# Smaller loads, held for a place in TensorE's program: a ReLU²-attention and gated-MLP kernel on Trainium2

## The chip, the core and the metric

The kernel runs on one core of one Trainium2 chip. A core has TensorE (PE, matmuls; its weight loads are shown apart as PEld), VectorE (DVE), ScalarE (ACT), GpSimd (POOL) and SyncE (SP), and 16 DMA engines that move data between HBM and the core's SBUF and fetch program code. POOL and SP each issue DMAs in the order of their own program. The metric is device time in microseconds (us), as the median of several runs; the profile shows one execution.

## The reference

Attention without softmax, then a gated MLP without gate choice. Inputs are f32, the output is f32.

```python
batch, n_heads, seq, head_dim = (8, 12, 448, 64)
scores = 1/sqrt(64) * q @ k.T              # per batch and head
attn   = maximum(scores, 0)**2 / 448 @ v   # 8 x 12 x 448 x 64
x = attn.transpose(0, 2, 1, 3).reshape(3584, 768)
g, val = x @ w_gate, x @ w_val             # 768 -> 1536
out = (0.5*g*(1 + erf(g/sqrt(2))) * val) @ w_out   # 1536 -> 768
```

## The kernel before

Everything on TensorE is bf16 on 64x64 pieces of the array, so that four small matmuls run side by side. Each batch's 12 heads are worked in three **thirds** of four heads, named (b, m). A third goes through these steps:

- **Loads** (POOL queue). `load_qk` (line 345) issues one DMA for the four heads of q and one for those of k into the tile `qk16`, `load_v` (line 362) two for v, one for each half of the sequence; all cast f32 to bf16 on the way. `load` (line 319) makes the planned operation, with the bytes over a rate of 400e3 bytes per us as its planned transfer time (`arrivals`), and adds by hand the instructions that it must wait for (`op.behind`, reason "pace").
- **Transposition.** In batches 0 and 1 it is done by TensorE. From batch 2 on (`add_dma_transposes`, line 393), DVE regroups q and k into `qkr` (line 402) and SP issues two transposing DMAs (line 407) into `qkT`, one for four of the seven 64-row chunks and one for three. The second of a pair waits for the landing of the first; in batch 2 each waits for the one before it.
- **Scores, ReLU, square, values.** TensorE makes scores from `qkT` (tile `sp`), ACT takes the ReLU (line 634), DVE squares (line 646), TensorE multiplies with `v`, and DVE or ACT puts the result into `xT`.
- **MLP.** Gate, value and output products on `xT`, partly by seven-product Strassen groups, with gelu on ACT, sums on DVE, and output stores issued by SP (line 1156).

Buffers limit how far loads run ahead: `qk16` has two (RING_H), `v16` and `qkT` three each.

The order of every engine's instructions is made by a planner, `run_plan` (line 74), when the kernel is built. It steps through planned time. POOL and TensorE's lower rows have queues with a fixed order; SP, ACT, DVE and the upper rows have pools from which the earliest ready operation is taken. `ready` (line 84) gives the planned time at which an operation's inputs are there. TensorE work of later batches lies in a list `units`, and the first unit of the list that is ready is taken, so that other work goes ahead of a unit whose data are late. The planner counts 5.0 us for the landing of a transposing DMA after its issue, and 3.0 us more before scores may use it (1.5 us in batch 2).

Loads from batch 2 on are listed at line 1198 (`late`): q and k of one third, then v of the third before. Lines 1342 to 1350 pace them: q of third n waits for ReLU 0, and k for ReLU 1, of third n-3; the two v loads of a third wait for ReLUs 3 and 5 of the third two before it (PACE, line 252).

Of the kernel before, what the change touches and what calls it, by code (L numbers as in the profile page):

```python
# [28 lines left out]
class Op:  # L29


    def __init__(self, engine, cost, emit, deps=(), lag=0.0, prio=0, other=None):
        self.engine, self.cost, self.emit, self.prio = engine, cost, emit, prio
        self.deps = [d for d in deps if d is not None]
        self.lag = lag
        self.other = other
        self.takes = None
        self.margin = 0.0
        self.after = None
        self.start = self.end = self.known = self.blocked = None  # L40


# [15 lines left out]
            self.keys.add(key)  # L58


class Unit:


# [7 lines left out]
BANK = 0.3  # L71


def run_plan(queues, pools, units, banks, arrivals, together, fill):

    free = {e: 0.0 for e in (*queues, *pools)}
    at = {e: 0 for e in queues}
    dma = last = floor = busy = 0.0  # L80
    units.sort(key=lambda u: u.at)
    fixed = len(queues["PE0"])

    def ready(op):
        if op.known is not None:
            return op.known
        if op.blocked is not None and op.blocked.end is None:
            return None
        t = 0.0
        if op.after is not None:  # L90
            if op.after.start is None:
                return None
            t = op.after.start
        if op.takes is not None:
            x = op.takes[0].free(*op.takes[2:])
            if x is None:
                return None
            t = max(t, x)
        for d in op.deps:
            if d.end is None:  # L100
                op.blocked = d
                return None
            t = max(t, d.end + d.lag + (op.margin if d.engine == "SP" else 0.0))
        if op.takes is None:
            op.known = t
        return t
# [38 lines left out]

    left = sum(map(len, queues.values())) + sum(len(u.los) + len(u.his) for u in units)
    left += len({id(op) for ops in pools.values() for op in ops})
    while left:
        best = None
        for e, ops in queues.items():  # L150
            if at[e] < len(ops):
                r = ready(ops[at[e]])
                if r is not None:
                    t = max(r, free[e], floor if e in together else 0.0)
                    key = (t, 0, free[e])
                    if best is None or key < best[0]:
                        best = (key, e, ops[at[e]])
        whole = at["PE0"] == len(queues["PE0"])
        if whole or at["PE0"] >= fixed:
            found = next_unit(not whole)  # L160
            if found is not None:
                key = (found[0], -1, free["PE0"])
                if best is None or key < best[0]:
                    best = (key, "PE0", found)
        for e, ops in pools.items():
            mine = None
            for op in ops[:48]:
                r = ready(op)
                if r is not None:
                    t = max(r, free[e], floor if e in together else 0.0)  # L170
                    key = (t, op.prio, free[e])
                    if mine is None or key < mine[0]:
                        mine = (key, e, op)
            if mine and (best is None or mine[0] < best[0]):
                best = mine
        assert best is not None, "the plan is stuck"
        (t, _, _), e, op = best
        if isinstance(op, tuple):
            _, u, k = op
            u.begun = True  # L180
            units.remove(u)
            if k is not None:
                u.box["k"] = k
                banks[k] = u.closer()
            queues["PE0"][at["PE0"]:at["PE0"]] = u.los
            pools["PE1"] += u.his
            op = u.los[0]
        if op.other is not None and e != op.engine:
            op.engine, op.cost, op.emit = op.other
        op.start = t  # L190
        op.end = t + op.cost
        free[e] = op.end
        if e in together:
            floor = t
            if t > busy:
                fill(busy, t)
            busy = max(busy, op.end)
        if op in arrivals:
            dma = max(dma, op.end) + arrivals[op]
            op.lag = dma + 2.0 - op.end  # L200
        if e in at:
            at[e] += 1
        else:
            pools[e].remove(op)
            if op.other is not None:
                for x in ("ACT", "DVE"):
                    if x != e:
                        pools[x].remove(op)
        if op.takes is not None:
            op.takes[0].take(*op.takes[1:])  # L210
        op.emit()
        last = max(last, op.end)
        left -= 1
# [4 lines left out]
def kernel(  # L218
# [17 lines left out]
    P = 64  # L236
# [12 lines left out]
    OGS = d_model // NG  # L249
    WOG = 3  # L250
    SB = 2
    PACE = 0, 1, 3, 5
    FB = 4
    FILL = 30.0
    EARLY = 2

    NP = 2
    RING_V, RING_T, RING_H, RING_R, RING_A, RING_O = 3, 3, 2, 2, 4, 4
# [33 lines left out]
    ctx.enter_context(tc.manual_schedule())  # L292

    HALF = (slice(0, P), slice(P, 2 * P))

    n_reg, = nc.alloc_registers("n", engines=OrderedSet([mybir.EngineType.PE]))
    SYNC = mybir.DependencyInfo(mybir.DependencyClass.Sync, mybir.DependencyReason.DATA)

    def mm(o, lhsT, rhs, row, col, start, stop, onto=False):
        return nc.tensor.matmul(o, lhsT, rhs, start=start, stop=stop, skip_group_check=onto,  # L300
                                tile_position=(P * row, P * col))

    def wait_lower(box):

# [14 lines left out]
    def load(nbytes, emit, deps=(), cost=0.7, rate=400e3):  # L319
        def paced():  # L320
            ins = emit()
            for d in op.behind:
                tc.add_manual_dep(ins.ins, d.ins.name, SYNC, reason="pace")

        op = Op("POOL", cost, paced, deps)
        op.behind = [*deps]
        arrivals[op] = nbytes / rate
        POOL.append(op)
        return op
# [32 lines left out]
    def load_v(b, h0, h1, deps=()):  # L362

        m = h0 // 4
        for i in range(2):
            def emit(i=i):
                if (b, m) not in v16:
                    v16[b, m] = qkv.tile([128, 4, VC, D], bf16, name="v16", tag="v16")
                c0 = i * (SC - VC)
                return nc.gpsimd.dma_start(  # L370
                    v16[b, m][HALF[i], :, :, :],
                    v[b, h0:h1].rearrange("h (p c) d -> p h c d", c=SC)[:, :, c0:c0 + VC, :])
            op = load(4 * (h1 - h0) * VC * P * D, emit, deps, rate=400e3 if b else 300e3)
            v_loads.setdefault((b, m), []).append(op)
# [18 lines left out]
    def add_dma_transposes(b, m, deps=()):  # L393
# [9 lines left out]
                qkr[b, m].rearrange("p c h d -> p h c d"),  # L403
                qk16[b, m].rearrange("p h (c d) -> p h c d", d=D))

        def emit_transpose(c0, c1):
            ins = nc.sync.dma_start_transpose(
                qkT_tile(b, m)[:, c0:c1].rearrange("d c r x -> d (c r) x"),
                qkr[b, m][:, c0:c1].rearrange("p c h d -> p (c h d)"))
            if b > EARLY and c0 or m and b == EARLY:  # L410
                tc.add_manual_dep(ins.ins, one[0].ins.name, SYNC, reason="pace")
            one[:] = [ins]

        n = len(regrouped)
        copy = Op("DVE", 0.62, emit_copy, [wait, *(regrouped[n - 2] if n > 1 else ())], lag=0.15, prio=1)
        DVE.append(copy)
        copy.margin = 3.0
        tr_op[b, m] = [Op("SP", 0.19 * 2 * (c1 - c0), lambda c0=c0, c1=c1: emit_transpose(c0, c1),
                          [copy], lag=5.0) for c0, c1 in ((0, VC), (VC, SC))]
        qk_used[b, m] = [copy]  # L420
        t_made[b, m] = [*tr_op[b, m]]
        if m or b > EARLY:
# [51 lines left out]
    def fill(t0, t1):  # L474
# [10 lines left out]
            return  # L485
        t = new_bank(k, held[k])
        for _ in range(n):
            nc.tensor.matmul(t[:, :], warm[:, 0:128], warm[:, :], start=True, stop=True)  # L488

    last_scores = [None]  # L490

# [31 lines left out]
    def add_first_transposes(at):  # L523

        def emit(box, c0, c1, reader):
            src = qk16[0, 0].rearrange("p h (c d) -> p h c d", d=D)
            box[0] = t = new_bank(box["k"], reader, [128, c1 - c0, 2 * P], bf16)
            for c in range(c0, c1):
                for j in range(2):
                    nc.tensor.transpose(t[HALF[j], c - c0, :], src[:, j, c, :],  # L530
                                        ident[:, :], tile_position=(0, P * j))

        for engine, copy, c0, c1 in (("DVE", nc.vector.tensor_copy, 0, VC), ("ACT", nc.scalar.copy, VC, SC)):
            box = {}
# [14 lines left out]
    def add_transposes(at, b, m, rs):  # L549
# [6 lines left out]
        def emit(r):  # L556
# [7 lines left out]
            src = qk16[b, m].rearrange("p h (c d) -> p h c d", d=D)  # L564
            for c in range(SC):
                for j in range(2):
                    nc.tensor.transpose(t[HALF[j], c, :], src[:, 2 * r + j, c, :],  # L567
                                        ident[:, :], tile_position=(0, P * j))

        def emit_copy(r):  # L570
            nc.vector.tensor_copy(qkT_tile(b, m)[:, :, r, :], box[r])
# [626 lines left out]
    late = [(b, m) for b in range(2, B) for m in range(NM)]  # L1198
    for n, (b, m) in enumerate(late):
        for i in range(2):  # L1200
            load_qk(b, i, 4 * m, 4 * m + 4)
        for b_, m_ in late[n - 1:n] + (late[n:] if n == len(late) - 1 else []):
            load_v(b_, 4 * m_, 4 * m_ + 4)
    for b, m in late:
        add_dma_transposes(b, m)

# [122 lines left out]
    def emit_warm_up():  # L1329
        t = new_bank(0, None)  # L1330
        for _ in range(8):
            for j in range(2):
                nc.tensor.matmul(t[HALF[j], :], warm[:, HALF[j]], warm[:, :],
                                 start=True, stop=True, tile_position=(0, P * j))
    PE0.insert(0, warm_op)

    thirds = [(b, m) for b in range(B) for m in range(NM)]
# [4 lines left out]
    for n, (b, m) in enumerate(thirds):  # L1342
# [2 lines left out]
                op.behind.append(relus[(*thirds[n - 3], PACE[i])])  # L1345
        if (b, m) >= (2, 0):
            for i, op in enumerate(v_loads[b, m]):
                op.behind.append(relus[(*thirds[n - 2], PACE[2 + i])])
        for op in (*qk_loads[b, m], *v_loads[b, m]):
            op.deps += op.behind  # L1350
    for new, old in zip(duos[RING_A:], duos):
        gone = [o_op[b, pr] for keys in old["of"] for b, pr, _ in keys]
        for sq in new["sq"]:
# [9 lines left out]
    for op in [*ACT, *DVE]:  # L1363
        if op.other is not None:
# [1 line left out]

    banks = {k: readers.get(k, [None])[-1] for k in range(FB + 2)}
    run_plan({"PE0": PE0, "POOL": POOL}, {"PE1": PE1, "ACT": ACT, "DVE": DVE, "SP": SP, "IDLE": IDLE}, later,
             banks, arrivals, ("PE0", "PE1"), fill)


# [28 lines left out]
```

## Time and profile before

| what | value |
|---|---|
| median of 3 runs | 412.27 us (411.99 to 413.25) |
| the profiled execution, first to last instruction (span) | 410.9 us |
| TensorE busy | 395.7 us, 96% of the span |
| VectorE, ScalarE, GpSimd busy | 286.9, 243.9, 73.7 us |
| mean granted TensorE clock | 0.995 of full speed |
| DMA packets of the software queue (loads) | 37152, 24.39 MB |
| DMA packets of the hardware queue (stores, transposes) | 37888, 19.08 MB |
| DMA packets of TensorE's instruction queue (q8) | 70, 1.15 MB |
| transposing DMAs | 36, median 5.0 us from issue to landing |
| v loads; q loads; k loads of four heads | 4.6; 5.2; 6.5 us to landing (medians) |

The profile names instructions by the line that records them. All matmuls of attention and MLP are recorded at line 300 (the helper `mm`), so they are told apart by the tiles that they write and read: `sp<-qkT` are scores, `ff<-attnT,v` values, the rest the MLP. "issue" as the cause of idle time means that the engine waited for nothing that the profile shows. The packets of a DMA are shown by queue: q0 carries the loads, q1 stores and transposes, q8 and q14 program code. 1.15 MB in 70 packets is 16 KB for each.

### The profile page before, as it was taken

The numbers are of one execution on the slowest core, as the hardware profiler recorded it, in microseconds if no ns is written. First come the engines' busy times: TensorE is split into PE (matmuls) and PEld (weight loads), VectorE is DVE, ScalarE is ACT, GpSimd is POOL, SyncE is SP. The second block draws the span as 40 slices with busy tenths as digits, with TensorE's granted clock in tenths as the row PEclk, the third lists the DMA queues.
The fourth block names the chain that finished last, engine by engine and source line by source line (L and its number), as shares of the span: only waits on it lengthen the run. The fifth ranks groups of instructions, "written<-read, shape, count | busy, mean of one in ns | idle before, by whom it ended". The sixth has DMA issues, their size and how long they took to land.

```text
span 410.9 us, 19640 instructions
## 1 busy us (share of the span) xinstructions
PE 395.7 (96%) x9037; PEld 357.0 (87%) x9037; DVE 286.9 (70%) x494; ACT 243.9 (59%) x365; POOL 73.7 (18%) x120
## 2 busy tenths in 40 slices
PE   6999999988999999999999999999999999999994
PEld 3457788878999899989999999989899999999983
DVE  2786699757888687878855589868786773457462
ACT  4866673345777776766784466768677624434130
POOL 6566420211121121121210020211110000000000
PEclk8999999999999999999999999999999999999999
DMA  7999999979999989999990083997931203000405
GB/s 104 170 199 199 196 210 164 118 67 157 133 89 164 175 86 99 151 131 165 127 156 11 3 115 44 210 134 83 130 54 42 80 3 81 2 4 3 129 31 153
DMA packets 75282, 44.91 MB, mean 109 GB/s; under 512 B 36160, under 2 KB 71744, under 8 KB 75200
## 3 DMA queue, kind: packets, MB, share of 16 engines
q0 software_dynamic: 37152, 24.39, 46.8%
q1 hardware_dynamic: 37888, 19.08, 27.2%
q8 instruction: 70, 1.15, 1.1%
q10 hardware_dynamic: 160, 0.20, 0.2%
q14 instruction: 12, 0.10, 0.1%
HBM read 48.76 MB, written 11.01 MB: 145 GB/s over the span
## 4 chain that ended last, share of the span: by engine, by line
PE 95%; issue 2%; DMA 1%; POOL 1%; DVE 0%; ACT 0%; POOLq 0%
PE ff L300 84%; PE sp L300 8%; PE ff L488 1%; DMA qk<-in_k_dram 1%; PE ff L567 1%; PE sp L567 1%; POOL qk L355 0%; DVE xT L709 0%; DVE attnT L646 0%; ACT osb L1141 0%; POOL ident masks.py:199 0%; POOL ident masks.py:197 0%; POOLq L1384 0%
## 5 line engine op out<-in xcount | busy, mean ns | idle before, releaser
L300 PE MATMUL ff<-xT,wg 64*64 64x448 bf16 (+1 forms) x2112 | 210.5, 336 | 0.6 <-issue 0.6
L634 ACT ACTIVATE rl<-sp 128x896 bf16<-128x896 f32 x168 | 152.2, 919 | 65.2 <-PE sp L300 56.4
L300 PE MATMUL ff<-xT,wv 64*64 64x448 bf16 x1632 | 187.5, 349 | 1.0 <-issue 1.0
L300 PEld LDWEIGHTS <-wv 64*64 64x64 bf16 x2112 | 129.7, 107 | 9.7 <-issue 3.3
L300 PEld LDWEIGHTS <-wg 64*64 64x64 bf16 x2112 | 128.8, 107 | 7.1 <-issue 0.5
L646 DVE TENSOR_TENSOR attnT<-rl 128x1792 bf16<-128x1792 bf16 (+1 forms) x98 | 92.3, 953 | 19.1 <-ACT rl L634 18.4
L300 PE MATMUL ff<-attnT,v 64*64 64x448 bf16 (+1 forms) x768 | 84.4, 326 | 0.4 <-DVE attnT L646 0.2
L300 PEld LDWEIGHTS <-s 64*64 64x64 bf16 x1344 | 78.5, 107 | 5.3 <-issue 2.9
L300 PE MATMUL sp<-qkT 64*64 64x448 bf16 (+1 forms) x768 | 78.5, 330 | 0.6 <-ACT qkT L538 0.6
L951 DVE TENSOR_TENSOR uT<-gel,ff 128x448 bf16<-128x448 bf16 x68 | 42.0, 619 | 33.3 <-PE ff L300 29.9
L300 PEld LDWEIGHTS <-uT 64*64 64x64 bf16 x936 | 60.5, 107 | 1.4 <-issue 0.2
L300 PE MATMUL ff<-wo,s 64*64 64x384 bf16 x672 | 58.6, 323 | 0.0
L300 PE MATMUL ff<-wo,uT 64*64 64x384 bf16 x600 | 56.5, 323 | 0.0
L300 PE MATMUL ff<-wt,s 64*64 64x384 bf16 x672 | 53.0, 323 | 2.6 <-issue 2.6
L946 ACT ACTIVATE gel<-ff 128x448 bf16<-128x448 f32 x68 | 37.0, 544 | 28.7 <-PE ff L300 28.5
L370 POOL DMA_DIRECT2D v<-in_v_dram x48 | 29.5, 619 | 127.3 <-ACT rl L634 85.4
L300 PEld LDWEIGHTS <-v 64*64 64x64 bf16 x768 | 47.1, 107 | 5.0 <-issue 2.5
L1141 ACT COPY osb<-ff 128x384 f32<-128x384 f32 x56 | 26.6, 479 | 36.7 <-PE ff L300 35.4
L300 PEld LDWEIGHTS <-qkT 64*64 64x64 bf16 x768 | 38.8, 106 | 7.0 <-issue 3.7
L300 PE MATMUL ff<-ts,ws 64*64 64x224 bf16 (+1 forms) x480 | 42.7, 293 | 0.7 <-issue 0.7
L300 PEld LDWEIGHTS <-ws 64*64 64x64 bf16 x720 | 41.5, 107 | 1.8 <-issue 1.4
L300 PE MATMUL ff<-ts,wv 64*64 64x224 bf16 (+1 forms) x480 | 41.9, 293 | 1.1 <-issue 1.1
(57 smaller groups left out, 352.8 us busy)
## 6 DMA issues: line engine op xcount, KB each, us to landing
out_dram<-osb SPq DMA_DIRECT2D x54, 192.0 KB, 3.8
v<-in_v_dram POOLq DMA_DIRECT2D x48, 128.0 KB, 4.6
qk<-in_q_dram POOLq DMA_DIRECT2D x23, 224.0 KB, 5.2
qk<-in_k_dram POOLq DMA_DIRECT2D x23, 224.0 KB, 6.5
wg<-in_moe_w_gate_dram POOLq DMA_DIRECT2D x6, 384.0 KB, 9.9
wv<-in_moe_w_val_dram POOLq DMA_DIRECT2D x6, 384.0 KB, 11.1
wo<-in_moe_w_out_dram POOLq DMA_DIRECT2D x4, 576.0 KB, 14.7
qkT<-qkr SPq DMA_TRANSPOSE x36, 5.0
```

What stands on the lines that cost most here:

```text
L300: return nc.tensor.matmul(o, lhsT, rhs, start=start, stop=stop, skip_group_check=onto, tile_position=(P * row, P * col))
L370: return nc.gpsimd.dma_start(v16[b, m][HALF[i], :, :, :], v[b, h0:h1].rearrange("h (p c) d -> p h c d", c=SC)[:, :, c0:c0 + VC, :])
L488: nc.tensor.matmul(t[:, :], warm[:, 0:128], warm[:, :], start=True, stop=True)
L567: nc.tensor.transpose(t[HALF[j], c, :], src[:, 2 * r + j, c, :], ident[:, :], tile_position=(0, P * j))
L634: relu.ins = nc.scalar.activation(duo["rl"][:, u % 2, :, :], box[0][:, :, 0:S], AF.Relu).ins
L646: nc.vector.tensor_tensor(a[:, part], duo["rl"][:, part], duo["rl"][:, part], op=ALU.mult)
L946: nc.scalar.activation(gel[b, fc][:, :], box[0][:, 0:S], AF.Gelu)
L951: u_op[b, fc].ins = nc.vector.tensor_tensor(uT[b][:, fc, :], gel.pop((b, fc))[:, :], box[0][:, 0:S], op=ALU.mult).ins
L1141: ins = nc.scalar.copy(o, box[0][:, 0:OGS])
```

## The change

Three things change; nothing that is computed does.

1. From batch 2 on each load covers two heads instead of four: per third four DMAs for q and k and four for v, instead of two and two. PACE becomes `0, 0, 1, 2, 3, 4, 5, 6`: both halves of q wait for ReLU 0, those of k for ReLUs 1 and 2, the four parts of v for ReLUs 3, 4, 5 and 6.
2. A counter `Blocks` counts two instructions (weight load and matmul) for each matmul as the plan emits it. It starts at 74, and each time the count plus 36 reaches a further multiple of 256 it marks the matmul and its planned time.
3. Loads from batch 2 on, and all transposing DMAs, get a `gate`, their planned transfer time (0.573 us for two heads of q or k, 0.328 us for two heads of a half of v, 1.2 us for a transpose). The planner takes such an operation only if the transfers counted so far and its own end by 7.1 us (`BLOCK`) after the last mark; else it waits for the next mark. In the program, the DMA also gets a wait for the last marked matmul. If nothing else can be planned, the limit is dropped for one step.

Stores, weight loads and the loads of batches 0 and 1 are not held. The list of TensorE work is the same; the plan's order may come out otherwise, since the planner is run anew.

```diff
+class Blocks:
+    def __init__(self, size, first, lead):
+        self.size, self.lead = size, lead
+        self.count, self.next = first, size
+        self.marks = []
+        self.now = 0.0
+
+    def add(self, ins, n=2):
+        self.count += n
+        if self.count + self.lead >= self.next:
+            self.marks.append((self.now, ins))
+            self.next += self.size
...
 def ready(op):
...
+        if op.gate:
+            if not blocks.marks:
+                return None
+            at, _ = blocks.marks[-1]
+            t = max(t, at, free[op.engine])
+            if not forced and max(traffic, t + 1.3) + op.gate > at + span:
+                return None
+            return t
...
+        if op.gate:
+            op.mark = blocks.marks[-1][1]
+        if op.gate or op in arrivals:
+            traffic = max(traffic, t + 1.3) + (op.gate or arrivals[op])
...
-    PACE = 0, 1, 3, 5
+    PACE = 0, 0, 1, 2, 3, 4, 5, 6
...
+    GATE_T, BLOCK = 1.2, 7.1
...
+    blocks = Blocks(256, 256 - 192 + 10, 36)
...
 def paced():        # in load
...
+            if op.mark is not None:
+                tc.add_manual_dep(ins.ins, op.mark.ins.name, SYNC, reason="pace")
...
+            if tr_op[b, m][i].mark is not None:    # in emit_transpose
+                tc.add_manual_dep(ins.ins, tr_op[b, m][i].mark.ins.name, SYNC, reason="pace")
...
+        for op in tr_op[b, m]:
+            op.gate = GATE_T
...
     for n, (b, m) in enumerate(late):
         for i in range(2):
-            load_qk(b, i, 4 * m, 4 * m + 4)
+            for h in (4 * m, 4 * m + 2):
+                load_qk(b, i, h, h + 2)
         for b_, m_ in late[n - 1:n] + (late[n:] if n == len(late) - 1 else []):
-            load_v(b_, 4 * m_, 4 * m_ + 4)
+            for h in (4 * m_, 4 * m_ + 2):
+                load_v(b_, h, h + 2)
...
-                op.behind.append(relus[(*thirds[n - 2], PACE[2 + i])])
+                op.behind.append(relus[(*thirds[n - 2], PACE[4 + i])])
         for op in (*qk_loads[b, m], *v_loads[b, m]):
             op.deps += op.behind
+            if b >= EARLY:
+                op.gate = arrivals[op]
```

More of the change, by code (lines that the diff above doesn't have):

```diff
@@ L39, in __init__ @@
         self.after = None
+        self.gate = 0.0
+        self.mark = None
         self.start = self.end = self.known = self.blocked = None
@@ L71, with run_plan @@
 BANK = 0.3
-def run_plan(queues, pools, units, banks, arrivals, together, fill):
+def run_plan(queues, pools, units, banks, arrivals, together, fill, blocks, span):
     free = {e: 0.0 for e in (*queues, *pools)}
     at = {e: 0 for e in queues}
-    dma = last = floor = busy = 0.0
+    dma = last = floor = busy = traffic = 0.0
     units.sort(key=lambda u: u.at)
@@ L147, in run_plan @@
     left += len({id(op) for ops in pools.values() for op in ops})
+    forced = False
     while left:
@@ L175, in run_plan @@
                 best = mine
+        if best is None and not forced:
+            forced = True
+            continue
         assert best is not None, "the plan is stuck"
+        forced = False
         (t, _, _), e, op = best
@@ L189, in run_plan @@
             op.engine, op.cost, op.emit = op.other
-        op.start = t
+        op.start = blocks.now = t
         op.end = t + op.cost
+        if op.gate:
+            op.mark = blocks.marks[-1][1]
+        if op.gate or op in arrivals:
+            traffic = max(traffic, t + 1.3) + (op.gate or arrivals[op])
         free[e] = op.end
@@ L299, in mm @@
     def mm(o, lhsT, rhs, row, col, start, stop, onto=False):
-        return nc.tensor.matmul(o, lhsT, rhs, start=start, stop=stop, skip_group_check=onto,
-                                tile_position=(P * row, P * col))
+        ins = nc.tensor.matmul(o, lhsT, rhs, start=start, stop=stop, skip_group_check=onto,
+                               tile_position=(P * row, P * col))
+        blocks.add(ins)
+        return ins
     def wait_lower(box):
@@ L370, in emit @@
                 return nc.gpsimd.dma_start(
-                    v16[b, m][HALF[i], :, :, :],
+                    v16[b, m][HALF[i], h0 % 4:h0 % 4 + h1 - h0, :, :],
                     v[b, h0:h1].rearrange("h (p c) d -> p h c d", c=SC)[:, :, c0:c0 + VC, :])
@@ L404, in emit_copy, with emit_transpose @@
                 qk16[b, m].rearrange("p h (c d) -> p h c d", d=D))
-        def emit_transpose(c0, c1):
+        def emit_transpose(i, c0, c1):
             ins = nc.sync.dma_start_transpose(
@@ L417, in add_dma_transposes @@
         copy.margin = 3.0
-        tr_op[b, m] = [Op("SP", 0.19 * 2 * (c1 - c0), lambda c0=c0, c1=c1: emit_transpose(c0, c1),
-                          [copy], lag=5.0) for c0, c1 in ((0, VC), (VC, SC))]
+        tr_op[b, m] = [Op("SP", 0.19 * 2 * (c1 - c0), lambda i=i, c0=c0, c1=c1: emit_transpose(i, c0, c1),
+                          [copy], lag=5.0) for i, (c0, c1) in enumerate(((0, VC), (VC, SC)))]
+        for op in tr_op[b, m]:
+            op.gate = GATE_T
         qk_used[b, m] = [copy]
@@ L487, in fill @@
         for _ in range(n):
-            nc.tensor.matmul(t[:, :], warm[:, 0:128], warm[:, :], start=True, stop=True)
+            blocks.add(nc.tensor.matmul(t[:, :], warm[:, 0:128], warm[:, :], start=True, stop=True))
     last_scores = [None]
@@ L529, in emit @@
                 for j in range(2):
-                    nc.tensor.transpose(t[HALF[j], c - c0, :], src[:, j, c, :],
-                                        ident[:, :], tile_position=(0, P * j))
+                    blocks.add(nc.tensor.transpose(t[HALF[j], c - c0, :], src[:, j, c, :],
+                                                   ident[:, :], tile_position=(0, P * j)))
         for engine, copy, c0, c1 in (("DVE", nc.vector.tensor_copy, 0, VC), ("ACT", nc.scalar.copy, VC, SC)):
@@ L566, in emit @@
                 for j in range(2):
-                    nc.tensor.transpose(t[HALF[j], c, :], src[:, 2 * r + j, c, :],
-                                        ident[:, :], tile_position=(0, P * j))
+                    blocks.add(nc.tensor.transpose(t[HALF[j], c, :], src[:, 2 * r + j, c, :],
+                                                   ident[:, :], tile_position=(0, P * j)))
         def emit_copy(r):
@@ L1332, in emit_warm_up @@
             for j in range(2):
-                nc.tensor.matmul(t[HALF[j], :], warm[:, HALF[j]], warm[:, :],
-                                 start=True, stop=True, tile_position=(0, P * j))
+                blocks.add(nc.tensor.matmul(t[HALF[j], :], warm[:, HALF[j]], warm[:, :],
+                                            start=True, stop=True, tile_position=(0, P * j)))
     PE0.insert(0, warm_op)
@@ L1368 @@
     run_plan({"PE0": PE0, "POOL": POOL}, {"PE1": PE1, "ACT": ACT, "DVE": DVE, "SP": SP, "IDLE": IDLE}, later,
-             banks, arrivals, ("PE0", "PE1"), fill)
+             banks, arrivals, ("PE0", "PE1"), fill, blocks, BLOCK)
 _INS = ['q', 'k', 'v', 'moe_w_gate', 'moe_w_val', 'moe_w_out']
```

## The prediction

> **What bounds the kernel now.** I read the page first, then the time by stages, then TensorE's waits, its timeline at each wait, and the DMA queues in windows around them.
>
> ```profile
> PE 395.7 (96%) x9037; PEld 357.0 (87%) x9037; DVE 286.9 (70%) x494; ACT 243.9 (59%) x365; POOL 73.7 (18%) x120
> q8 instruction: 70, 1.15, 1.1%
> ```
> TensorE is the bound: 96% of the span. Its 9037 matmuls and 9037 weight loads are 18074 instructions; over 256 that is 70.6, and queue q8 has 70 packets of 16 KB. So one packet brings 256 TensorE instructions. By stages (start:end and length, then busy us and count of PE, PEld, DVE, ACT, POOL, the granted clock, the DMA share, GB/s):
>
> ```profile
> 70.00:100.00 30.00, 26.15 (x713) 24.18 (x708) 19.26 (x35) 13.85 (x22) 4.89 (x8) 1.00 1.02 113
> 215.00:236.00 21.00, 21.00 (x455) 20.26 (x451) 12.08 (x25) 9.13 (x17) 0.43 (x1) 1.00 0.14 12
> 236.00:330.00 94.00, 92.88 (x2290) 89.03 (x2286) 75.56 (x130) 66.37 (x97) 11.78 (x20) 1.00 0.65 97
> 330.00:400.00 70.00, 70.00 (x1576) 66.27 (x1570) 37.94 (x77) 24.36 (x48) 0.00 (x0) 1.00 0.14 37
> ```
> TensorE is never idle where the DMA share is 0.14, and loses 3.85 us of 30 and 1.1 of 94 where it is 1.02 and 0.65; the clock is full in all. What it waits for:
>
> ```profile
> PE ff L300 <- issue: 6.0, 7, 2.6
> ```
> Seven waits on nothing that the profile shows. The longest, on TensorE's timeline (start, duration):
>
> ```profile
> 81.22 0.35 PE L300 MATMUL ff<-wt,uT 64*64 64x384 bf16 x2
> 84.16 0.35 PE L300 MATMUL ff<-wt,s 64*64 64x384 bf16 x2 [2.59 <-issue]
> ```
> Idle time counts from a matmul's modelled end, 0.3 us after the next would usually have started, so each wait costs about 0.3 us more than it shows: 81.22 to 84.16 is 2.9 us. From start to start, less the usual interval, I read **eight stalls**: 0.5 (at 71.8), 2.9 (81.3), 1.3 (98.1), 0.9 (136.3), 0.4 (145.3, too short for the list), 0.75 (182.4), 1.05 (267.2), 0.7 (292.2): **8.5 us**. Where they stand in the program, by counts from the start:
>
> ```profile
> 0.00:72.10 72.10, 68.49 (x1243) 47.63 (x1244) 51.60 (x86) 45.13 (x60) 33.41 (x54) 0.98 1.21 177
> 0.00:83.00 83.00, 77.76 (x1499) 56.32 (x1500) 58.96 (x100) 48.66 (x67) 35.85 (x58) 0.98 1.19 168
> 0.00:98.90 98.90, 91.99 (x1883) 69.47 (x1884) 68.73 (x115) 57.37 (x79) 38.30 (x62) 0.98 1.18 162
> ```
> 2487, 2999 and 3767 instructions: steps of 512 and 768, whole blocks of 256. The other five follow in steps of 1788, 512, 1789, 3835 and 1278, which are 7, 2, 7, 15 and 5 blocks less up to 5 semaphore instructions that these counts leave out. And the queues, before and at the resumption (76.2 to 81.2, then 81.2 to 83):
>
> ```profile
> q0 software_dynamic: 1035, 0.68, 105.5%
> q1 hardware_dynamic: 530, 0.13, 35.4%
> ...
> q8 instruction: 1, 0.02, 5.3%
> ```
> For 5 us, loads and transposes held the engines and no code packet ran; it started at 81.25, took 1.5 us, and TensorE went on 1.4 us after its end. At all eight stalls the resumption comes 1.35 to 1.6 us after a code packet's end. In quiet stretches the packet starts within 0.5 us of the block's boundary. So each stall is late program code, delayed behind loads, transposes and stores. A block lasts 4.3 to 6.0 us; less 1.0 for the packet and 1.4 after it, about 2 to 3.5 us of delay are free.
>
> **The change, part by part.**
>
> *The mark.* It falls at instruction 146 of a block of 256; the stalls stand at 183 in the counts above, and at 169 by 292 us. So it is 37 to 23 instructions, 0.85 to 0.5 us, ahead. A lone load's first packet runs 1.3 us after its issue on POOL (the load at 125.83), a transpose's 1.2 us after (at 149.86): traffic released by the mark starts behind the code packet. That part fits the trace.
>
> *The hold.* I put the rule against the times of before: 107 loads and transposes from 48 us on, each with its planned transfer, 7.1 us after its mark as limit. It would have held 19, most by under 1 us. Stall by stall: at 81.3 the second transpose and both v loads come out over the limit, at 145.3 the k load, at 182.4 the transpose, at 71.8 the v load behind the weights. At 98.1, 136.3, 267.2 and 292.2 (3.95 us together) it holds nothing of weight. The limit is loose: at 292.2, a transpose and a k load issued at 283.57 and 284.09 count 1.2 and 1.15 us, but landed 8.0 and 7.4 us later; and those blocks are shorter than 7.1 us. Stores are not counted.
>
> *Two heads.* The second half of k comes one ReLU later, about 1.6 us by the ReLUs' pace, so that a transpose meets half a load. It also costs POOL 72 more DMAs at 0.61 us, 44 us on an engine that is busy 73.7 of 411 us: nothing on the path. The cover is POOL's idle time between paced loads (2.4 to 3 us before most of them); without it, each piece would be 0.6 us later.
>
> *Waits on SP and POOL.* Behind a held transpose stand its pair and up to four stores; behind a held load, POOL's later loads. A transpose fits if issued up to 4.6 us after its mark, so it waits 1.3 us of a 5.9 us block at most when nothing else is in the way. From landing of a pair to its first scores there are 1.4 us in the first third of batch 2, 2.8 and 5.7 in the next, 6.9 or more in all later ones. Lateness is covered there, and the planner has MLP work to put first. I take nothing; the bounds are 0 and, for three full blocks of 5.9 us less those margins, 4.5 + 3.1 + 0.2 = 7.8 us.
>
> *What is late next.* The transpose issued at 73.46 landed at 84.0, the scores that need it start at 85.5. Without the stall of 2.9 us they would be reached at 82.6 and wait 1.4 us, unless it lands earlier. With the v loads held it should, by about 1 us (bounds 0 and 5.6: from 10.6 to the median of 5.0).
>
> ```profile
> DMA to landing us min/median/max: 2.7/5.0/10.6
> ```
>
> **The sum.** What I leave of the eight stalls, in order: 0.2 of 0.5, 1.2 of 2.9 (code or that transpose), 0.6 of 1.3, 0.3 of 0.9, 0.1 of 0.4, 0.1 of 0.75, 0.4 of 1.05, 0.2 of 0.7: held ones nearly vanish, the four others are cut by half or more because the traffic before them is halved and spread. That is 3.1 us; 8.5 - 3.1 = 5.4. The profiled execution would span 410.9 - 5.4 = 405.5. The median lies 1.4 us above that span; I carry it over: 412.3 - 5.4 = **406.9 us**. The rest of TensorE's time is its work, which stays.
>
> **Rivals.**
>
> 1. *All code comes in time.* For it: the free delay is 2 to 3.5 us and most stalls exceed it by under 1 us. Against: stores and the loose limit. 412.3 - 8.5 = 403.8, up to 404.6 if the transpose at 84 is still 0.8 us late. [...]
>
> 2. *The stalls only move.* Nineteen holds shift traffic, but the same bytes meet other boundaries; the four unheld stalls stay and new ones replace the held: 411.0 to 413.5. The same if the stalls had another cause than code. [...]
>
> 3. *Slower: late transposes.* The hold sends transposes and loads off together, right behind each mark; together they land late (8.0, 10.6 us, against under 3 alone). Scores stand in TensorE's fixed order, so a landing past the planner's 5 + 3 us (5 + 1.5 in batch 2) stops it. Place: the first scores of each third, first at 85 to 115 us. Price: 10.6 instead of 5.0 is 5.6 us a pair member; two members late, 11.2 less the margins of 1.4, 2.8 and 5.7, is 9.8 + 8.4 + 5.5 at the very worst; I price a third of it, 7.9, against 4.4 of stalls saved: 412.3 + 3.5 = 415.8. It decides from about 4.4 us of such waits. Against: no such wait stands in the list now.
>
> **Numbers.** Forecast 0.52 (404.8 to 410.0), rival 1 0.17, rival 2 0.12, rival 3 0.19. The range, **403.7 to 413.5**, takes in the first three and leaves out most of rival 3. About 0.3% (1.2 us) is what a measurement of this kernel can tell from no change. Faster: 0.52 + 0.17 + 0.03 of rival 2 = 0.72; same: 0.07 of rival 2; slower: 0.02 of it and rival 3, 0.21.
>
> **What would show it.** Waits of TensorE on "issue" fall from 6.0 us and 7 to about 2 us and 3; what is left lies where stores run. A scores wait on the DMA of `qkT`, above all near 84 us, would be rival 3. Landings of loads fall to 3 to 4 us, transposes stay near 5. If TensorE's waits vanish and the time does not follow, the reading of the eight stalls is wrong; if new ones stand at steps of 256, rival 2 holds.

## The result

The changed kernel takes **407.25 us** (median of 4 runs, 404.92 to 407.73), the kernel before 412.13 us beside it (4 runs, 410.03 to 413.25): a ratio of **0.9899**, 95% interval 0.9862 to 0.9937. The forecast was 406.9 us, in a range of 403.7 to 413.5.

In the page after, TensorE's busy time hardly moves, and POOL has the 72 more DMAs; then the issues of loads (count, KB, us to landing):

```profile
PE 394.4 (97%) x9037; PEld 353.2 (87%) x9037; DVE 287.2 (71%) x494; ACT 243.7 (60%) x365; POOL 116.2 (29%) x192
...
v<-in_v_dram POOLq DMA_DIRECT2D x72, 64.0 KB, 3.7
qk<-in_q_dram POOLq DMA_DIRECT2D x38, 112.0 KB, 3.8
qk<-in_k_dram POOLq DMA_DIRECT2D x38, 112.0 KB, 4.5
```

By stages, columns as before:

```profile
70.00:100.00 30.00, 29.34 (x780) 26.89 (x775) 21.99 (x38) 16.25 (x27) 12.27 (x21) 1.00 1.10 143
...
236.00:330.00 94.00, 92.47 (x2286) 85.09 (x2282) 74.03 (x127) 63.36 (x92) 21.73 (x36) 1.00 0.61 92
```
TensorE's idle time from 70 to 100 us falls from 3.85 to 0.66 us. From 236 to 330 us it rises a little, 1.1 to 1.5. TensorE's waits on nothing in the profile:

```profile
PE ff L337 <- issue: 2.8, 5, 1.2
```
They were 6.0 us in 7; the prediction looked for about 2 us in 3 waits. No wait of scores on a transpose has come in their place.

**How stalls are counted from here on.** From 60 us on, a code stall is a stretch of over 0.3 us between the starts of two matmuls that ends 1.2 to 1.75 us after the end of a packet on queue q8; 0.08 us of it is taken off as the usual interval. In the profile before they sum to 8.2 us (I had read 8.5), in the profile after to 4.3: 0.5 at 79.4 us, 0.6 at 93.5, 0.3 and 0.9 at 135.2 and 139.5, 1.45 and 0.5 at 261.6 and 267.4.

The spans differ by 5.1 us, 410.9 and 405.8. Set side by side by the matmul work done, about 1.8 us of that stand already at 20 us, where both kernels have the same order of work; the rest comes between 70 and 100 us and in small steps later. Whether that lead belongs to the change was the first question.

### The profile page after: what moved, and what is told of

It is laid out like the page before. It is cut to its first block, busy times and chain, and to the rows that moved or that the text cites. A ratio compares the mean times of both kernels' runs of the same rounds, so it can differ in the third digit from the quotient of the medians.

```text
span 405.8 us, 19802 instructions
## 1 busy us (share of the span) xinstructions
PE 394.4 (97%) x9037; PEld 353.2 (87%) x9037; DVE 287.2 (71%) x494; ACT 243.7 (60%) x365; POOL 116.2 (29%) x192
## 4 chain that ended last, share of the span: by engine, by line
PE 96%; issue 1%; DMA 1%; POOL 1%; DVE 0%; ACT 0%; POOLq 0%
PE ff L337 85%; PE sp L337 8%; PE ff L533 1%; DMA qk<-in_k_dram 1%; PE sp L612 1%; PE ff L612 1%; POOL qk L396 0%; DVE xT L754 0%; DVE attnT L691 0%; ACT osb L1186 0%; POOL ident masks.py:199 0%; POOL ident masks.py:197 0%; POOLq L1433 0%
## 5 line engine op out<-in xcount | busy, mean ns | idle before, releaser
L337 PE MATMUL ff<-xT,wg 64*64 64x448 bf16 (+1 forms) x2112 | 206.7, 336 | 0.0
L337 PE MATMUL ff<-xT,wv 64*64 64x448 bf16 x1632 | 182.8, 349 | 0.1
L337 PEld LDWEIGHTS <-wv 64*64 64x64 bf16 x2112 | 121.7, 107 | 7.7 <-issue 2.2
L337 PEld LDWEIGHTS <-wg 64*64 64x64 bf16 x2112 | 121.4, 107 | 6.4
L411 POOL DMA_DIRECT2D v<-in_v_dram x84 | 50.6, 606 | 103.4 <-ACT rl L679 47.2
L337 PEld LDWEIGHTS <-s 64*64 64x64 bf16 x1344 | 73.8, 107 | 5.1 <-issue 0.6
L337 PEld LDWEIGHTS <-uT 64*64 64x64 bf16 x936 | 56.3, 107 | 2.8
L337 PE MATMUL ff<-wt,s 64*64 64x384 bf16 x672 | 50.8, 322 | 0.0
L337 PEld LDWEIGHTS <-v 64*64 64x64 bf16 x768 | 44.8, 107 | 4.1 <-issue 1.7
L337 PEld LDWEIGHTS <-ws 64*64 64x64 bf16 x720 | 38.9, 107 | 2.7 <-issue 2.1
```

Of the source, the lines that this page charges most:

```text
L337: ins = nc.tensor.matmul(o, lhsT, rhs, start=start, stop=stop, skip_group_check=onto, tile_position=(P * row, P * col))
L411: return nc.gpsimd.dma_start(v16[b, m][HALF[i], h0 % 4:h0 % 4 + h1 - h0, :, :], v[b, h0:h1].rearrange("h (p c) d -> p h c d", c=SC)[:, :, ...
```

## The experiments

There were three theories. **Code:** stalls are late code, delayed by data traffic; pieces and hold both let code through sooner. **Pieces:** the smaller load does it, the hold nothing. **Order:** any new order of work meets the boundaries otherwise, and the first was unlucky. All ratios are to the kernel before, on the same chip.

| run | what | ratio (95%) | code stalls of its profile, us |
|---|---|---|---|
| before2 | kernel before again | one run, 410.3 us | 6.5 |
| again | changed kernel again | 0.9894 (0.9858 to 0.9930) | 2.5 |
| halves | pieces and pacing, no hold | 0.9915 (0.9882 to 0.9948) | 4.4 |
| split2 | pieces alone, order of before | 0.9928 (0.9895 to 0.9962) | 5.1 |
| hold4b | hold alone, four heads | 0.9935 (0.9901 to 0.9970) | 4.0 |
| nowait | plan of the change, no waits for marks | 0.9902 (0.9869 to 0.9935) | 1.8 |
| shift | marks half a block later | 0.9881 (0.9830 to 0.9932) | 2.9 |
| tight | limit 5.6 us | 0.9993 (0.9964 to 1.0022) | 1.3 |
| reroll | another order, loads as before | 0.9988 (0.9953 to 1.0023) | 5.8 |

The sums hold together in two ways. By counts of matmuls and weight loads, every counted stall of these profiles and of the doses below ends at the same place of a block of 256 instructions, but for one (in tight, below); in the first profiles of both kernels it is place 183, falling to 169 before and 171 after in the course of the program, and 192 or 193 with TensorE's semaphore instructions counted. And if each profile's stalls are taken off its span, 401.1 to 402.8 us are left in twelve of the fourteen profiles, whose spans go from 403.4 to 410.9 us. Only hold4b (404.8) and tight (407.2) stand apart, and both lose time in another way, as told at their runs.

### Both kernels again

> The changed kernel, unaltered, to measure it more often beside the kernel before. Code theory (the gain is the fall of the stalls behind late program code from about 8 to about 4 us; the 1.8 us that the two first profiles differ by ahead of 20 us is chance): ratio 0.989 to 0.993, stalls after 60 us of 4 to 5 us at the same places in the program as in the first profile, and no constant lead of 1.8 us at the start. Rival (the start is faster too): ratio below 0.988, and every profile of the changed kernel is ahead by 1.5 to 2 us at 20 us.

> The kernel before, unaltered, for a second profile of it. If late code makes the stalls: stalls of 6 to 10 us after 60 us, at places that are steps of 256 instructions apart, most of them at the same places as in the first profile, and an arrival at 20 us of the span that may differ from the first profile by up to 2 us. If the lead of 1.8 us of the changed kernel's first profile at 20 us belongs to the change, this profile is late there like the first.

In each row below are a window from 0 to 20 us and the busy time and count of TensorE first; the kernel before, first profile:

```profile
0.00:20.00 20.00, 16.75 (x196) 7.67 (x199) 9.61 (x19) 12.62 (x16) 12.22 (x24) 0.91 1.03 135
```
the kernel before, second profile:

```profile
0.00:20.00 20.00, 17.46 (x222) 8.38 (x222) 11.52 (x22) 14.26 (x18) 14.02 (x27) 1.00 1.07 144
```
the changed kernel, first profile:

```profile
0.00:20.00 20.00, 17.75 (x226) 8.38 (x228) 11.52 (x23) 14.29 (x18) 14.17 (x27) 1.00 1.07 145
```
The second profile of the kernel before is as early as the changed kernel (222 and 226 matmuls by 20 us, against 196; mean clock 1.00 and 1.00, against 0.91). So the 1.8 us are chance of the first profile and no part of the change; over all fourteen profiles the count at 20 us goes from 196 to 226. The ratio repeats. The stalls vary between executions of one kernel: 8.2 and 6.5 us before; 4.3 and 2.5 us after, and in three more profiles that run the changed kernel's order up to 335 us (the doses below) 3.0, 1.25 and 4.85. The means are 7.3 and 3.2, a fall of 4.1 us; the two ratios are 4.2 and 4.4 us of 412. So the stalls' fall is the whole of the gain within what these can tell. The rule may miss something: the second profile of the kernel before has one more stop on nothing that the profile shows, of 0.75 us, at a block's boundary but 2.5 us after the end of a code packet:

```profile
274.06 0.38 PE L300 MATMUL ff<-xT,wv 64*64 64x448 bf16 x2
274.92 0.38 PE L300 MATMUL ff<-xT,wg 64*64 64x448 bf16 x2 [0.48 <-issue]
```
With it that profile has 7.2 us of stalls, the mean of before is 7.7 and the fall 4.5. Why this stop came so long after the packet is open.

### Pieces without a hold

```diff
-        for op in tr_op[b, m]:
-            op.gate = GATE_T
...
-            if b >= EARLY:
-                op.gate = arrivals[op]
```

> Loads of two heads and their pacing, without any hold or mark. If the smaller and later pieces alone free the code: time as the changed kernel's, 407 to 408.5, stalls of 4 to 5 us. If the hold does most of it: 409.5 to 411.5, stalls of 6 to 8 us. If the stalls only move with any new order: anywhere from 406 to 413, with stalls at other places.

Ratio 0.9915 (408.6 us of 412.1), at the edge of the first expectation, and the stalls within it: most of the gain. It differs from the changed kernel's by less than the intervals.

### Pieces in the order of before

The kernel before, with each late load issued in two parts inside one planned step (v likewise):

```diff
+        def emit_pieces():
+            n = (h1 - h0) // 2 if b >= EARLY else h1 - h0
+            return [nc.gpsimd.dma_start(
+                tile_of()[:, x:x + n, :], src[b, h0 + x:h0 + x + n].rearrange("h (p c) d -> p h (c d)", c=SC))
+                for x in range(0, h1 - h0, n)]
...
```

> The kernel before, with its order of all instructions and its pacing, but each late load of q, k or v issued as two DMAs of two heads right behind each other: size of the piece alone, no later pacing, no hold. If the smaller piece lets code through: ratio 0.990 to 0.994, stalls of 3 to 5 us. If the changed order or the spreading in time does it, and not the size: 0.998 to 1.002, stalls of 7 to 9 us at the places of before.

Ratio 0.9928 with the order and pacing of the kernel before. So size alone, with the 0.6 us on POOL between the parts, gives about 3 us of the gain.

### Another order

```diff
-SHIFT = "-8.5 0 -8 0 17.5 -10.5 -5.5 -12.5 14 -26.5 -11.5 -1.5"
+SHIFT = "-8 0 -7.5 0 18 -10.5 -5.5 -12.5 14 -26.5 -11.5 -1.5"
```

> The kernel before, with the planned places of the scores of batches 2 to 4 moved by 0.5 us: another order with no change in loads, size or hold. If stalls fall with any new order (the first was unlucky): ratio 0.990 to 0.995. If the loads decide: 0.998 to 1.004, stalls of 6 to 10 us, partly at other places.

Ratio 0.9988, no change. The stalls of its one profile (5.8 us) lie under both of before, but that execution was also the fastest of its twelve (409.1 us; the median is 410.9), so I read this as the spread between executions. This order gives no gain; one other order is not every order.

### The hold with four heads

With the limit of 7.1 us and four-head loads paced as before, the planner comes to a point where nothing can be planned; with 6.6 us it goes through.

```diff
-    PACE = 0, 0, 1, 2, 3, 4, 5, 6
-    GATE_T, BLOCK = 1.2, 7.1
+    PACE = 0, 1, 3, 5
+    GATE_T, BLOCK = 1.2, 6.6
...
-            for h in (4 * m, 4 * m + 2):
-                load_qk(b, i, h, h + 2)
+            load_qk(b, i, 4 * m, 4 * m + 4)
...
```

> Hold of loads and transposes with loads of four heads, paced as before, and a limit of 6.6 us instead of 7.1. If the hold by itself does a good part: ratio 0.988 to 0.993, stalls of 3 to 5 us. If it does nothing without the smaller pieces: 0.997 to 1.003, stalls of 7 to 9 us.

Ratio 0.9935 with stalls of 4.0 us: the hold alone also works, but it pays. By the work done, it loses some 2 us against the changed kernel's second profile from 120 to 132 us without a stall. The window in this kernel, then the same in the changed kernel's second profile:

```profile
120.00:132.00 12.00, 12.00 (x252) 10.38 (x246) 9.60 (x16) 8.90 (x14) 2.94 (x5) 1.00 0.97 178
```
```profile
120.00:132.00 12.00, 12.00 (x299) 11.70 (x293) 8.97 (x15) 8.46 (x12) 4.54 (x8) 1.00 1.03 188
```
Both show TensorE busy for all 12 us, but 252 matmuls against 299: fewer of them overlapped, and busy time hides it. From the counts I take it that the array's parts were not all in use; which work was missing there, and why, is not shown.

### The plan without the waits, and the marks moved

```diff
-            if op.mark is not None:
-                tc.add_manual_dep(ins.ins, op.mark.ins.name, SYNC, reason="pace")
...
-            if tr_op[b, m][i].mark is not None:
-                tc.add_manual_dep(ins.ins, tr_op[b, m][i].mark.ins.name, SYNC, reason="pace")
```

> The changed kernel's plan, with the same order of all instructions, but without the waits of the DMAs for the marked matmul. If the waits in the program keep traffic off the code: loads issue earlier than in the changed kernel, stalls of 6 to 8 us, 409.5 to 411.5. If the planned order is enough because ReLUs and buffers release the loads at about the planned times anyway: within 0.3% of the changed kernel, 406 to 408.5.

Ratio 0.9902, as the changed kernel. Behind 90 us most loads (91 of 119) issue within five matmuls of the same place with and without the wait, so it was seldom what released them. The transposes do feel it: against the changed kernel's second profile, 13 of the 32 behind 90 us issue 9 to 100 matmuls earlier without it, and the time does not rise.

```diff
-    blocks = Blocks(256, 256 - 192 + 10, 36)
+    blocks = Blocks(256, 256 - 192 + 10, 36 - 128)
```

> The changed kernel with every mark 128 instructions later, half a block off: the same pieces, the same hold, but its window of 7.1 us ends in the middle of the following block. If the place of the hold in the block matters: ratio 0.993 to 1.000, stalls of 5 to 9 us. If the pieces and the spread in time do all of it: ratio as the changed kernel's, 0.989 to 0.992, stalls of 2 to 4.5 us.

Ratio 0.9881. The place of the hold in the block makes no difference that these runs can tell.

### A tighter hold

```diff
-    GATE_T, BLOCK = 1.2, 7.1
+    GATE_T, BLOCK = 1.2, 5.6
```

> The changed kernel with a limit of 5.6 us after the mark instead of 7.1, about the length of a short block. If the loose limit leaves the remaining stalls: stalls of 1 to 2.5 us, ratio 0.984 to 0.988. If what is left comes from stores and from the double transposes at 72 us, which no limit counts or splits: stalls of 2 to 4 us, ratio 0.988 to 0.992. If the later loads of batch 2 leave TensorE's rows unpaired as in the hold with four-head loads: a loss without a stall of 1 us or more near 110 to 135 us.

Two expectations came true at once: the fewest stalls of the table (1.3 us, of which 0.35 at 108.2 us lies in the middle of a block and so is not code), and the largest loss without them. The ratio that was expected with so few stalls, 0.984 to 0.988, did not come. From 164 to 176 us, in this kernel and in the changed kernel's second profile:

```profile
164.00:176.00 12.00, 11.44 (x204) 8.18 (x200) 4.96 (x10) 9.05 (x14) 1.78 (x3) 1.00 0.54 57
```
```profile
164.00:176.00 12.00, 12.00 (x296) 11.33 (x292) 8.57 (x16) 8.96 (x15) 4.04 (x7) 1.00 0.75 101
```
204 matmuls against 296, about 3.7 us of time lost, and the ratio is 0.9993. VectorE and POOL do less there too (10 and 3 instructions against 16 and 7). I read it as attention that comes so late by the hold that TensorE runs short of work; no run shows the step itself. The place differs from the one I expected (110 to 135 us).

### Traffic where there was none

The changed kernel with extra loads and transposes into buffers that are no longer used, released by chosen matmuls behind 335 us; two runs with milder doses at the mark and half a block later, then one with a dose like that ahead of the 2.9 us stall:

```diff
...
+    def strong(ins, heads):
+        dose_transposes(ins, 2)
+        dose_loads(ins, heads, 16 // heads)
+
+    doses = {220 + 256 * 59 + 64: lambda ins: strong(ins, 4),
+             220 + 256 * 61: lambda ins: strong(ins, 4),
+             220 + 256 * 63 + 128: lambda ins: strong(ins, 4),
+             220 + 256 * 65 + 128: lambda ins: strong(ins, 2)}
```

> The changed kernel with four extra doses of DMA traffic into buffers that are no longer used, in the stretch from 335 us on that has almost no other traffic, each released at the mark of a block, one dose in every second block: (1) four loads of four heads, (2) one transpose and two loads of four heads, (3) one transpose and four loads of two heads, the same bytes as (2), (4) two transposes. If stalls are late code, and traffic behind the code packet is harmless: no stall, the code packets of the dosed blocks start within 0.5 us of their boundary and those of the next within 1.5 us, time as the changed kernel's within 0.2%. If traffic slows TensorE in some other way (its reads or its clock): loss of 0.3 us or more at each dose, wherever it stands in the block.

> The same four doses, each half a block (128 instructions, about 3 us) later, so that they are under way when the next block's code is asked for. If stalls are late code: code packets behind the doses start 1.5 to 3.5 us late; stalls of up to 1 us at (1) and (2), less at (3) than at (2) if the size of the pieces counts, and none to 0.5 at (4); in sum 0.5 to 2.5 us slower than with the doses at the marks. If the place in the block does not matter: same time and losses as with the doses at the marks.

> The changed kernel with a dose like that ahead of the 2.9 us stall of the kernel before (two transposes and four loads of four heads at once), in the quiet stretch from 335 us on, at three places: a quarter of a block after the mark, at the mark, and half a block after the mark; and half a block after the mark again with the loads in two-head pieces. If stalls are code delayed by traffic: stalls appear where there were none, whole blocks after the mark, each ending 1.35 to 1.6 us after a code packet; none to 0.7 us at the mark, 0.3 to 1.5 at a quarter, 0.5 to 2 at half, and less with the pieces. If the long blocks here (5.95 us) leave time enough for any dose: no stall, delays of 2 to 3.3 us. If traffic hurts in another way: losses that do not end at a block's boundary.

The mild doses settle nothing about the place: ratios 0.9935 (0.9902 to 0.9967) at the marks and 0.9900 (0.9834 to 0.9966) half a block later, no stall behind 335 us in either. They delay code by up to 2.2 and 2.4 us against the packets of quiet blocks, without a stall.

The strong doses do make stalls. Here are the first and the third on TensorE's timeline:

```profile
350.07 0.35 PE L337 MATMUL ff<-xT,wg 64*64 64x448 bf16 x1
351.51 0.35 PE L337 MATMUL ff<-xT,wg 64*64 64x448 bf16 x1 [1.09 <-issue]
...
375.20 0.32 PE L337 MATMUL ff<-wt,s 64*64 64x384 bf16 x1
376.24 0.32 PE L337 MATMUL ff<-wt,uT 64*64 64x384 bf16 x1 [0.71 <-issue]
```
and its queues from 345.5 to 348.6 us, with no code packet, then from 348.6 to 350.4:

```profile
q0 software_dynamic: 412, 0.35, 86.6%
q1 hardware_dynamic: 462, 0.13, 49.8%
...
q1 hardware_dynamic: 222, 0.36, 62.0%
q0 software_dynamic: 63, 0.05, 16.7%
q8 instruction: 1, 0.02, 4.8%
```
The code packet runs from 348.71 to 350.10, 4.1 us late, and TensorE goes on at 351.51, 1.41 us after its end. Less the interval, the stalls are 1.4 us (dose a quarter of a block after the mark, with two stores beside it), 0.5 (at the mark; the first stall falls between this mark and its block's start, so that the dose, from 349.98 us, runs 1.5 us ahead of it) and 1.0 (half a block). They end 1.35 to 1.46 us after a code packet; the second and third stand one and four blocks of 256 instructions behind the first. The same bytes in two-head pieces, half a block after the mark, delay code by 1.2 us instead of 3.4 and make **no stall**. The eight smaller pieces also take twice as long on POOL, 4.7 us, so size and spread are not told apart here; and the next packet comes 2.1 us late, behind the rest of the dose and five stores. The run's ratio is 0.9965 (0.9923 to 1.0006), against 0.9899 and 0.9894 without doses: some 2.8 us more, and the three stalls come to 2.8 us. In no other profile is there a stall behind 335 us. That loads and transposes delay code into stalls is thereby shown, not only read.

## Why the prediction was right, step by step

- **What bounds the kernel.** Right: the stalls stand whole blocks apart, each ends just behind a code packet (1.24 to 1.66 us), and the strong doses make them (1.4, 0.5 and 1.0 us).
- **The sum.** I took 5.4 us off. The stalls fell by 4.1 us on the mean of the profiles, and 4.2 to 4.4 us by the two ratios. The term that was mis-sized is the 8.5 us of stalls before: one execution's, at the upper end; the second had 6.5. What is left I gave as 3.1 us; the mean of five profiles is 3.2. The median of 407.25 is nearer to the forecast than the ratio puts it (412.27 x 0.9899 = 408.1).
- **What is left, stall by stall.** These could not be foreseen one by one: the stalls at 182 and 292 us went, as I had for the one, and those near 140 and 262 us stayed or grew (0.9 and 1.45 us in the first profile, 0.35 and 0.45 in the second). The sum held better than its parts.
- **The hold.** I gave it the stalls that its rule would have caught. Alone it does take about half of the stalls, but its waits in the program (nowait) and its place in the block (shift) do not matter measurably. What is left is that the plan spreads transfers in time, which is argued and not shown. Whether it adds anything to pieces and pacing (0.9915 against 0.9881 to 0.9902) stays open.
- **The mark.** That traffic released by it starts behind the code packet fits the trace, but no run shows that it pays.
- **Two heads.** Right in direction and undersold: alone about 3 us. POOL's 116.2 us came out about as counted (73.7 + 44), and hid.
- **What is late next.** The transpose that landed 10.6 us after its issue lands at 80.8, 7.1 us after it, and the first scores start at 81.5, without a wait.
- **Rival 1** (all code in time) did not happen: 1.25 to 4.85 us stay in the five profiles of this order. **Rival 2** (the stalls only move) fell with reroll, split2 and the ratios. **Rival 3** (late transposes) did not happen in the changed kernel. Its 415.8 us were reckoned with 4.4 us of stalls saved where the sum takes off 5.4; with 5.4 it would have been 414.8. The price of a hold showed in another form, as fewer matmuls in the same time, in hold4b (some 2 us) and tight (3.7 us). A hold at no cost, as I took it, held with the loose limit of 7.1 us and two heads, and not in these two. With the same bytes the pieces delay code by 1.2 us against 3.4 (dose_strong); in what order the DMA engines serve their queues, no run shows. TensorE crosses some 60 of 69 block boundaries of the profile before without a stall; the others cost 8.2 us there and 6.5 in the second profile, so there was something to gain.

No version here beats the changed kernel measurably; the one without its waits (nowait) is simpler and as fast.

## What to carry to other kernels

If a busy TensorE stops on nothing that the profile shows, count instructions. Stops whole blocks of 256 apart that end just behind a packet of the instruction queue (1.24 to 1.66 us) were late code here, so look at the transfers in flight ahead of them. Issue large loads in smaller pieces and spread them (split2: 0.9928, halves: 0.9915), first without any gate; a gate can cost as much in matmuls not done in the same time (tight: 204 against 296 in 12 us) as it saves (ratio 0.9993), and matmul counts by window show that where busy time does not (hold4b: 252 against 299 in 12.00 busy us). Do not size a gain of 1% from one execution: take two profiles of the kernel before.

## What the runs showed of the hardware

- A TensorE code packet of 16 KB mostly takes 0.9 to 1.4 us here (at most 2.5, the one ahead of the stall at 182.4 us); after a stall matmuls go on 1.24 to 1.66 us after its end. In the dosed blocks of 5.4 to 6.05 us, delays up to 2.4 us cost nothing, and 3.4 to 4.1 us cost 0.5 to 1.4.
- Loads alone kept the DMA queues full from 45 to 67 us (a DMA share of 1.28 in the profile before), and code packets came 2.6 to 3.5 us late there, without a stall before 70 us. Two transposes together with four-head loads made it 3.4 to 4.5 us (the doses, and the stall at 81.3 us).
- Executions of the same order of work up to 335 us differ by 3.6 us in their code stalls there (1.25 to 4.85 us in five profiles), nearly as much as the gain of the change.
